# Left-over scores of an attention kernel: one form for all batches, and another place in the first batch

## The chip, the cores and the metric

The kernel runs on one core of a Trainium2 chip. The metric is the device time of that core in microseconds, as the median of several runs. One execution was also recorded by the hardware profiler; it is the profiled execution of the tables and quoted lines below. Times inside it are counted from the start of its span.

## The reference

Attention with a relative position bias, followed by a feed-forward layer with three first matrices whose products go through a maximum:

```python
scores = scale * np.matmul(q, k.transpose(0, 1, 3, 2))      # 8 batches, 8 heads, 576 x 64
scores = scores + bias.transpose(2, 0, 1)[None, :, :, :]     # a table's entry by |row - column|
scores = scores - np.max(scores, axis=-1, keepdims=True)
attn = np.exp(scores)
attn = attn / (np.sum(attn, axis=-1, keepdims=True) + 1e-09)
attn_out = np.matmul(attn, v)
x = attn_out.transpose(0, 2, 1, 3).reshape(B * S, H * D)     # 4608 x 512
h = np.maximum(np.maximum(x @ w1, x @ w2), x @ w3)           # 4608 x 768
out = h @ w_out
```

## The kernel before

**Units of work.** The eight heads are taken as four pairs (`hp`, 0 to 3). A head has 576 positions: four tiles of 128, and 64 left over. Scores are held transposed, with keys on the partitions. For a pair there are four pieces:

- *two visits* (`visit`, line 554), c = 0 for queries 0 to 255 and c = 1 for queries 256 to 511, each against the 512 keys of the four whole tiles. A visit makes two score tiles `sc`, and ACT turns each into a piece of `e4` with one exponential of 1024 columns (line 539);
- *the left-over keys* (`left_keys`, line 573): the last 64 keys of both heads against all queries, tile `sct`, into `el`;
- *the left-over queries*: the last 64 queries against the 512 keys, eight matmuls of 64 columns into `scq`, into the other part of `el`. There are two forms. `left_queries` (line 589) puts them in one tile of the pool `ps_s` and makes one exponential of 512 columns. A visit that is given `el` does them ahead of its own scores, in two tiles of the pool `ps_a`, with two exponentials of 256 columns.

The bias is multiplied in afterwards on DVE, as exp(bias): `times_band` for `e4`, `times_bandt` and `times_band_left` for `el`. Then `attend` (line 604) multiplies with the values, in two halves of the queries; the function that it returns does the division on DVE (`quotients`, lines 638 to 651) into `x_sb`. The list `late` holds the attends that are still to do, and `next_late` takes the first.

**Banks.** PSUM is split into three pools of two tiles each. `ps_s` (tiles of two banks) holds `sc`, `sct`, `scq` of the first form, and `tp` of `second_transposes`. `ps_a` holds the tiles of `attend`, and `scq` of the second form. `ps_f` holds the feed-forward tiles `ps` and `pso`, and the turnings `xp` and `tp2`. A new tile of a pool waits until what was in its place has been read.

**Order.** Matmuls and transposes are issued through helpers (lines 93 to 97) that keep them in program order on TensorE, so that one that waits holds up all behind it. Most DVE work is kept in order likewise. Feed-forward work for 512 tokens is cut into portions (`ffn`, line 317) in the list `pending`, and `fill(target, *hooks)` (line 439) issues portions whose sizes, in matmuls of 512 columns, sum to at most `target` (at least one portion), with the hooks between them: with one hook, it is called ahead of the last group; with two, they are spread. A portion of size 4 for the 256-token halves of batch 0 is eight matmuls of 256 columns, a block `ps`.

**Batch 0** runs in two passes over the pairs: first all visits c = 0, then (lines 758 to 810) all visits c = 1 with the left-overs and the bands. In this second pass the turnings of x (`x_transposes`, line 654: PE transposes into `xp`, one ACT copy to `xT`) make the transposed rows that the feed-forward work reads.

**Batches 1 to 7** (lines 813 to 894) do for each pair: visit c = 0; the attend of the first half of the pair before; a fill with the left-over keys; visit c = 1; a second fill. For batch 1 the turned queries and keys of the next pair are made by `second_transposes` (line 507) right after visit c = 1, as ten PE transposes into `tp` and four copies on DVE and ACT; later batches get them from the DMA queue of SP (`transposes`, line 454). The flag `together` (line 818) is true from batch 2, pair 1 on. Where it is true, the left-over queries are done in visit c = 1 (second form), the attend of the second half is done in the first fill right behind the left-over keys, and the first product of a block in the second fill takes its bank from `ps_a` (`idle_sums`, line 339). Where it is false, `left_queries` is called in the second fill, and the attend of the second half stands behind visit c = 1 (lines 860 to 863). `rate` is 8 for batch 1 and pair 0 of batch 2, and 13 after.

Of the kernel before, what the change touches and what calls it, by code (L numbers as in the profile page):

```python
# [39 lines left out]
def kernel(  # L40
# [19 lines left out]
    HP = H // 2  # L60
    QS = 2 * P
    QM = 2 * QS
# [28 lines left out]
    inorder = tc.keep_in_program_order  # L91
# [325 lines left out]
    pending, rest, stores, deferred, idle_sums = [], [], [], [], []  # L417
# [6 lines left out]
    def add_ffn(t0, nt, last=False):  # L424
        portions, left = ffn(t0, nt, last)
        portions[0] = rest + portions[0]
        rest[:] = left
        pending.extend((sum(n for n, _ in p), [fn for _, fn in p]) for p in portions)
# [10 lines left out]
    def fill(target, *hooks):  # L439

        groups, spent, hooks = [], 0, list(hooks)
        while pending and (not groups or spent + pending[0][0] <= target):
            n, fns = pending.pop(0)
            spent += n
            groups += [fn for fn in fns if fn]
        for j, group in enumerate(groups):
            while hooks and (j == len(groups) - 1 or j > 0 and len(hooks) > len(groups) - 1 - j):
                hooks.pop(0)()
            group()
        for hook in hooks:  # L450
            hook()
# [55 lines left out]
    def second_transposes(made, hp):  # L507

        hs = slice(2 * hp, 2 * hp + 2)
        tp = ps_s.tile([P, 2, 2 * CH], BF16, tag="sc", name="tp")  # L510
        for j, tl in enumerate((qtail, ktail)):
            for t in range(KT):
                tr(tp[:, j, P * t : P * t + P], batch[1][j][:, t, hs, :].rearrange("p h d -> p (h d)"), ident[:])
            tr(tp[:, j, KT * P : KT * P + P], tl[1][:, hp, :], ident[:])
        main = [
            copy(
                made[j][:, hp, 0 : KT * P].rearrange("c (p t) -> c p t", t=KT),
                tp[:, j, 0 : KT * P].rearrange("c (t p) -> c p t", t=KT),
            )
            for j, copy in enumerate((dve_copy, act_copy))  # L520
        ]
        tail = [
            copy(made[j][:, hp, KT * P :], tp[:, j, KT * P : n])
            for j, (copy, n) in enumerate(((dve_copy, S), (act_copy, (KT + 1) * P)))
        ]
        other_banks([main[1], tail[1]], [main[0], tail[0]])
        other_banks([tail[0]], [main[1]])

    def times_band(hp, e4, t, lo, hi, put=lambda x: x):
        lo, hi = max(lo, P * t - P), min(hi, P * t + 2 * P)  # L530
        if lo < hi:
            c0, c1 = BAND - (hi - P * t + P), BAND - (lo - P * t + P)
            put(nc.vector.tensor_tensor(  # L533
                out=e4[:, t, :, lo:hi], in0=e4[:, t, :, lo:hi],
                in1=hank[:, 2 * hp : 2 * hp + 2, c0:c1][:, :, ::-1], op=ALU.mult,
            ))
# [117 lines left out]
    def x_transposes(hp, half):  # L654

        xp = ps_f.tile([P, 2 * CH], BF16, tag="ff", name="xp")
        lo, hi = (0, QS) if half == 0 else (QS, S)
        for q in range(lo // P, -(-hi // P))[::-1]:
            c = min(P * q, S - P) - lo
            tr(xp[:, c : c + P], x_sb[0][:, q, P * hp : P * hp + P], ident[:])  # L660
        act_copy(xT[:, hp, lo:hi], xp[:, 0 : hi - lo])
# [8 lines left out]
    def next_late():  # L670
        return late.pop(0)() if late else (lambda: None)
# [9 lines left out]
    qk = [qk_tiles(), qk_tiles()]  # L681
# [45 lines left out]
    for hp in range(HP):  # L727
        qT, kT = (x[:, hp, :] for x in qk[0])
        e4, el = e_tiles()
# [28 lines left out]
    for hp in range(HP):  # L758
        qT, kT = (x[:, hp, :] for x in qk[0])
        e4, el = e_tiles()  # L760
        visit(qT, kT, e4, 1, (lambda: more_transposes(hp + 1)) if hp + 1 < HP else None)
        if hp == 0:
            bands(HP - 2)
            bands(HP - 1)
        if hp == 1:
            x_transposes(0, 0)
        if hp == 2:
            x_transposes(2, 0)
            x_transposes(3, 0)
            add_ffn(0, QS)  # L770

        def keys():
            left_keys(hp, qT, kT, el, QS, S)

        def queries():
            left_queries(hp, qT, kT, el)

        if hp == 0:
            keys()
            queries()  # L780
        quotients = next_late()

        def late_bands():
            for t in range(KT):
                times_band(hp, e4, t, QS, QM, inorder)

        if hp < 2:
            quotients()
            if hp == 1:
                keys()  # L790
            if hp == 1:
                x_transposes(1, 0)
            quotients = next_late()
            if hp == 1:
                queries()
            quotients()
            if hp == 0:
                make_bandt()
            late_bands()
            products(hp, el)  # L800
        else:
            if hp == HP - 1:
                batch[2] = load_tiles()
                load_qk(2)
                x_transposes(0, 1)
            quotients()
            late_bands()
            fill(8, keys, queries, *([lambda: second_transposes(qk[1], 0)] if hp == HP - 1 else []))
            products(hp, el)
        late.append(lambda hp=hp, e4=e4, el=el: attend(0, hp, e4, el, 1))  # L810

    turned = [lambda hp=hp: x_transposes(hp, 1) for hp in range(1, HP)]
    for b, hp in [(b, hp) for b in range(1, B) for hp in range(HP)]:
        if hp == 0:
            x_sb[b] = x_tile()
        qT, kT = (x[:, hp, :] for x in qk[b])
        e4, el = e_tiles()
        together = b > 1 and (b, hp) != (2, 0)
        rate = 8 if b == 1 or (b, hp) == (2, 0) else 13

        visit(qT, kT, e4, 0)
        store_outputs()
        if b == 1:
            if hp == 0:
                crossbar = transposes(2)
            next(crossbar, None)
        elif hp and b + 1 < B:
            if hp == 1:  # L830
                crossbar = transposes(b + 1)
            next(crossbar)
        early()
        if turned:
            turned.pop(0)()
        quotients = next_late()
        times_band(hp, e4, 0, 0, QS, inorder)
        quotients()
        if b == 1 and hp + 1 < HP:
            spread_packed(hp + 1, nc.vector)  # L840
        if (b, hp) == (1, 1):
            add_ffn(QS, QS)

        def keys():
            left_keys(hp, qT, kT, el, 0, S)
            if together:
                next_late()()

        fill(rate, keys, *([lambda: None] if together else []))
        times_bandt(hp, el)  # L850


        visit(qT, kT, e4, 1, el=el if together else None)
        store_outputs()
        if b == 1 or hp in (1, 2) and b + 1 < B:
            next(crossbar, None)
        early()
        if turned:
            turned.pop(0)()
        if not together:  # L860
            quotients = next_late()
            times_band(hp, e4, 1, 0, QM, inorder)
            quotients()
        if b == 1 and hp + 1 < HP:
            second_transposes(qk[1], hp + 1)
        if hp == 1 and b > 1:
            add_ffn((b - 1) * CH, CH)
        if hp == (2, 2, 0)[min(b, 3) - 1] and b + 1 < B:
            if b == 1:
                load_last_weights(turned_qk[2, 1, 1])  # L870
            load_v(b + 1, 0, H, turned_qk[b + 1, 1, KT - 1] if b < 3 else None)
        if (b, hp) == (2, 0):
            batch[3] = load_tiles()
            load_qk(3, divided[1, HP - 1, 1])
        if hp == 2 and 1 < b < B - 2:
            batch[b + 2] = load_tiles()
            load_qk(b + 2, turned_qk[b + 1, 1, KT - 1])

        def queries():
            if not together:  # L880
                left_queries(hp, qT, kT, el)
            times_band(hp, e4, 3, 0, QM, inorder)

        def bands_2():
            for t in range(1 if together else 2, 3):
                times_band(hp, e4, t, 0, QM, inorder)

        if together:
            idle_sums.append(hp)
        fill(rate, bands_2, queries)  # L890
        idle_sums.clear()
        times_band_left(hp, el)
        for half in range(2):
            late.append(lambda b=b, hp=hp, e4=e4, el=el, half=half: attend(b, hp, e4, el, half))
# [44 lines left out]
```

## Time and profile before

| What | Value |
|---|---|
| Median of 10 runs | 319.91 us (319.37 to 322.19) |
| The profiled execution | 319.97 us |
| Its span, first to last instruction | 318.2 us |
| Granted TensorE clock, mean of the span | 0.995 |
| PE, matmuls | 303.5 us busy, 95% |
| DVE | 213.5 us, 67% |
| ACT | 201.2 us, 63% |
| POOL | 108.2 us, 34% |
| One exponential of a score tile, 128 x 1024 | 1029 ns, 128 of them |

The page gives, for each engine, its busy time and a row of 40 digits, the busy share of 40 equal slices of the span in tenths (one slice is 8 us). The chain that ended last follows the work back from the last instruction. In the timeline a row has its start, how long it took from first to last, the engine and line, what it writes and reads (out<-in), the shape, the number of instructions merged into it, and in brackets idle time before it with what ended it. Matmuls overlap in such rows, so two starts tell more than the duration. In rows of windows come the stretch, its length, the busy time of PE, weight loads, DVE, ACT and POOL, then the granted clock of TensorE, the share of DMA and the rate.

Where the pieces lie: the second pass of batch 0 from about 20 to 35 us, batch 1 from 34.7, batch 2 from 62.5, its pair 1 from 68.6 and its pair 2 from 75.6 us.

### The profile page before, as it was taken

How to read it: one execution, taken by the hardware profiler on the slowest of the kernel's cores; microseconds unless marked ns; L12 is line 12 of the kernel's file. 1: busy time of each engine (PE TensorE's matmuls, PEld its weight loads, DVE VectorE, ACT ScalarE, POOL GpSimd, SP SyncE). 2: the span in 40 equal slices, each digit the busy share in tenths (PEclk: the TensorE clock that was granted, in tenths of full speed). 3: DMA queues.
4: the chain of work that ended last, by engine and by line, in shares of the span. 5: the costliest groups of instructions: out<-in, count | busy, mean ns of one | idle time of the engine just before them, and what ended most of it. 6: DMA issues, size and time to landing. Idle time of an engine off the chain costs nothing.

```text
span 318.2 us, 8198 instructions
## 1 busy us (share of the span) xinstructions
PE 303.5 (95%) x3288; PEld 171.4 (54%) x3328; DVE 213.5 (67%) x535; ACT 201.2 (63%) x297; POOL 108.2 (34%) x143
## 2 busy tenths in 40 slices
PE   7778999999999999999999999999999999999995
PEld 2356777775555555555555555555555555444442
DVE  7476778777666766666666777767767775553552
ACT  4868988886777667767777677767776741122221
POOL 8948731447079502940195058300000000000000
PEclk9979999999999999999999999999999999999999
DMA  9999999999999999999999999994032103302103
GB/s 165 177 214 201 181 150 132 148 106 167 235 124 141 135 202 128 132 110 197 151 130 136 216 139 140 123 192 108 10 69 99 36 2 74 134 0 75 58 0 132
DMA packets 163878, 40.34 MB, mean 127 GB/s; under 512 B 153720, under 2 KB 159360, under 8 KB 163840
## 3 DMA queue, kind: packets, MB, share of 16 engines
q0 software_dynamic: 103776, 16.66, 79.4%
q1 hardware_dynamic: 58304, 22.69, 39.5%
q10 hardware_dynamic: 1760, 0.47, 0.7%
q8 instruction: 26, 0.43, 0.6%
q14 instruction: 12, 0.10, 0.1%
HBM read 35.39 MB, written 9.45 MB: 141 GB/s over the span
## 4 chain that ended last, share of the span: by engine, by line
PE 73%; issue 1%; DMA 1%; ACT 1%
PE ps L94 39%; PE pso L94 13%; PE a L94 11%; PE sc L94 7%; PE sct L94 2%; PE scq L94 2%; DMA out_dram<-osb 1%; ACT e L539 0%; ACT osb L388 0%; ACT osb L107 0%
## 5 line engine op out<-in xcount | busy, mean ns | idle before, releaser
L94 PE MATMUL ps<-xT,w_bf 128*128 128x512 bf16 (+1 forms) x693 | 148.7, 357 | 1.4
L539 ACT ACTIVATE e<-sc 128x1024 bf16<-128x1024 f32 x128 | 124.4, 1029 | 20.0 <-PE sc L94 17.5
L94 PEld LDWEIGHTS <-w_bf 128*128 128x128 bf16 x720 | 65.3, 98 | 62.7 <-issue 5.0
L533 DVE TENSOR_TENSOR e<-e,hank 128x512 bf16<-128x512 bf16 (+2 forms) x136 | 58.6, 467 | 12.1 <-ACT e L539 9.9
L345 ACT ACTIVATE m<-ps 128x512 bf16<-128x512 f32 x48 | 29.2, 608 | 51.9 <-PE ps L94 51.9
L354 DVE TENSOR_TENSOR m<-ps,m 128x512 bf16<-128x512 f32 x48 | 33.1, 689 | 34.1 <-PE ps L94 34.0
L94 PEld LDWEIGHTS <-kT 64*128 64x128 bf16 (+1 forms) x832 | 29.9, 95 | 36.8 <-issue 23.9
L94 PE MATMUL pso<-wo_bf,hT 128*128 128x512 bf16 (+2 forms) x209 | 47.8, 373 | 0.8 <-issue 0.2
L94 PE MATMUL a<-vx,e 128*128 128x65 bf16 x1024 | 45.9, 195 | 0.0
L360 DVE TENSOR_TENSOR hT<-ps,m 128x512 bf16<-128x512 f32 x48 | 33.0, 689 | 15.9 <-PE ps L94 14.4
L94 PE MATMUL sc<-qT,kT 64*128 64x256 bf16 x512 | 40.8, 272 | 2.9 <-ACT e L539 1.3
L94 PEld LDWEIGHTS <-e 128*128 128x128 bf16 x1024 | 41.6, 99 | 0.8
L167 POOL DMA_DIRECT2D q_sb<-in_q_dram x24 | 22.0, 918 | 49.8 <-DMA qT<-qtail 16.0
L94 PE MATMUL a<-vt,el 128*128 128x130 bf16 x160 | 35.8, 224 | 0.2 <-DMA vt<-in_v_dram 0.2
L139 POOL DMA_DIRECT2D vx<-in_v_dram x32 | 28.4, 914 | 22.0 <-PE ps L94 18.9
L110 DVE COPY osb<-pso 128x512 f32<-128x512 f32 (+1 forms) x33 | 22.6, 686 | 17.9 <-PE pso L94 14.7
L539 ACT ACTIVATE el<-scq 128x256 bf16<-128x256 f32 (+1 forms) x55 | 20.5, 416 | 19.7 <-PE scq L94 19.6
L641 DVE TENSOR_TENSOR x_sb<-a,rd 128x256 bf16<-128x256 f32 (+1 forms) x64 | 31.4, 491 | 2.2
L94 PEld LDWEIGHTS <-hT 128*128 128x128 bf16 x222 | 20.2, 98 | 22.3 <-issue 1.5
L94 PEld LDWEIGHTS <-el 128*128 128x128 bf16 x416 | 24.2, 97 | 9.4 <-issue 5.5
L539 ACT ACTIVATE el<-sct 128x576 bf16<-128x576 f32 (+2 forms) x36 | 21.7, 607 | 5.6 <-PE sct L94 4.2
L167 POOL DMA_DIRECT2D k_sb<-in_k_dram x24 | 22.0, 917 | 1.1 <-DMA w_bf<-in_moe_w_dram 1.1
(71 smaller groups left out, 168.9 us busy)
## 6 DMA issues: line engine op xcount, KB each, us to landing
out_dram<-osb SPq DMA_DIRECT2D x35, 256.0 KB, 3.1
vx<-in_v_dram POOLq DMA_DIRECT2D x32, 128.0 KB, 8.2
q_sb<-in_q_dram POOLq DMA_DIRECT2D x26, 128.0 KB, 5.4
k_sb<-in_k_dram POOLq DMA_DIRECT2D x24, 128.0 KB, 5.7
w_bf<-in_moe_w_dram POOLq DMA_DIRECT2D x3, 768.0 KB, 10.0
xT<-in_k_dram SPq DMA_DIRECT2D x6, 128.0 KB, 5.0
hank<-w_dr SPq DMA_DIRECT2D x2, 384.0 KB, 6.7
wo_bf<-in_moe_w_out_dram POOLq DMA_DIRECT2D x1, 768.0 KB, 8.2
```

What stands on the lines that cost most here:

```text
L94: inorder(nc.tensor.matmul(*args, **kw))
L110: return inorder(nc.vector.tensor_copy(out_, in_))
L139: in_turn(b, nc.gpsimd.dma_start(out=dst[:, t, h0:h1, :], in_=x[:, t, h0:h1, :])) for t in range(t0, t1)
L167: loads.append(in_turn(b, nc.gpsimd.dma_start(out=dst[:, t], in_=main_part(src, b)[:, t])))
L345: nc.scalar.activation(out=st[fb]["m0"][:], in_=ps0, func=ACTF.Copy)
L354: inorder(nc.vector.tensor_tensor(out=m[:], in0=ps1, in1=st[fb]["m0"][:], op=ALU.max))
L360: inorder(nc.vector.tensor_tensor(out=block(fb), in0=ps2, in1=other, op=ALU.max))
L533: put(nc.vector.tensor_tensor(out=e4[:, t, :, lo:hi], in0=e4[:, t, :, lo:hi], in1=hank[:, 2 * hp : 2 * hp + 2, c0:c1][:, :, ::-1], op=ALU. ...
L539: nc.scalar.activation(out=out_, in_=in_, func=ACTF.Exp, scale=inv_sqrt_d)
L641: divided[b, hp, half] = inorder(nc.vector.tensor_tensor(out=x_sb[b][:, 2 * half : 2 * half + n, P * hp : P * hp + P].rearrange("p t (h d) ...
```

## The change

In batch 0's second pass: for pair 1, the left-over queries are done right behind the left-over keys, ahead of the turning of x and the attend that stood between. For pairs 2 and 3, left-over keys and queries leave the fill and come right behind the attend, ahead of the bands, of the turnings of x, and of the added feed-forward work (pair 2) or the loads of batch 2 (pair 3).

In batches 1 and 2: the flag `together` is gone, and what it stood for is done for all pairs. So batch 1, and pair 0 of batch 2, do the left-over queries in visit c = 1, and the attend of the second half in the first fill. The band of tile 1 (`times_band(hp, e4, 1, ...)`) moves from behind visit c = 1 to the hook of the second fill. The first fill of batch 2, pair 1, has the target 8 instead of 13.

```diff
@@ second pass of batch 0
-        if hp == 1:
-            x_transposes(0, 0)
-        if hp == 2:
-            x_transposes(2, 0)
-            x_transposes(3, 0)
-            add_ffn(0, QS)
...
         if hp == 0:
             keys()
             queries()
+        if hp == 1:
+            x_transposes(0, 0)
         quotients = next_late()
...
         if hp < 2:
             quotients()
             if hp == 1:
                 keys()
-            if hp == 1:
+                queries()
                 x_transposes(1, 0)
             quotients = next_late()
-            if hp == 1:
-                queries()
             quotients()
...
         else:
+            keys()
+            quotients()
+            queries()
+            late_bands()
+            if hp == 2:
+                x_transposes(2, 0)
+                x_transposes(3, 0)
+                add_ffn(0, QS)
+                fill(8)
+            else:
-            if hp == HP - 1:
                 batch[2] = load_tiles()
                 load_qk(2)
                 x_transposes(0, 1)
-            quotients()
-            late_bands()
-            fill(8, keys, queries, *([lambda: second_transposes(qk[1], 0)] if hp == HP - 1 else []))
+                fill(8, lambda: second_transposes(qk[1], 0))
             products(hp, el)
@@ batches 1 to 7
-        together = b > 1 and (b, hp) != (2, 0)
...
         def keys():
             left_keys(hp, qT, kT, el, 0, S)
-            if together:
-                next_late()()
+            next_late()()
 
-        fill(rate, keys, *([lambda: None] if together else []))
+        fill(8 if (b, hp) == (2, 1) else rate, keys, lambda: None)
         times_bandt(hp, el)
-        visit(qT, kT, e4, 1, el=el if together else None)
+        visit(qT, kT, e4, 1, el=el)
...
-        if not together:
-            quotients = next_late()
-            times_band(hp, e4, 1, 0, QM, inorder)
-            quotients()
...
         def queries():
-            if not together:
-                left_queries(hp, qT, kT, el)
             times_band(hp, e4, 3, 0, QM, inorder)
 
         def bands_2():
-            for t in range(1 if together else 2, 3):
+            for t in range(1, 3):
                 times_band(hp, e4, t, 0, QM, inorder)
 
-        if together:
-            idle_sums.append(hp)
+        idle_sums.append(hp)
```

More of the change, by code (lines that the diff above doesn't have):

```diff
@@ L776, in queries, with late_bands @@
             left_queries(hp, qT, kT, el)
+        def late_bands():
+            for t in range(KT):
+                times_band(hp, e4, t, QS, QM, inorder)
         if hp == 0:
@@ L780 @@
             queries()
+        if hp == 1:
+            x_transposes(0, 0)
         quotients = next_late()
-        def late_bands():
-            for t in range(KT):
-                times_band(hp, e4, t, QS, QM, inorder)
         if hp < 2:
```

## The prediction

> **What bounds the kernel now.** I read the page first, for the engine that is busy to the end and for the stretch in which it is not full.
>
> ```profile
> span 318.2 us, 8198 instructions
> ...
> PE 303.5 (95%) x3288; PEld 171.4 (54%) x3328; DVE 213.5 (67%) x535; ACT 201.2 (63%) x297; POOL 108.2 (34%) x143
> ...
> PE   7778999999999999999999999999999999999995
> ...
> ACT  4868988886777667767777677767776741122221
> ...
> PE 73%; issue 1%; DMA 1%; ACT 1%
> ```
>
> TensorE is the bound: nine tenths or more from 32 us on, and the chain that ended last is PE for 73% of the span, unbroken from 75 us. No later wait would hide a microsecond lost or won before that. Everything that the diff touches lies between 22 and 76 us, where ACT is nearly as full as PE. So I took the timeline of PE through it, and looked for starts further apart than the matmuls between them explain. A matmul of 64 rows by 256 columns runs beside its partner, and a pair takes 0.11; a 256-column `ps` takes 0.11, a transpose 0.06.
>
> ```profile
> 37.61 0.39 PE L94 MATMUL sc<-qT,kT 64*128 64x256 bf16 x4
> 38.19 0.40 PE L94 MATMUL sc<-qT,kT 64*128 64x256 bf16 x4 [0.19 <-ACT el L539]
> ...
> 52.87 0.66 PE L94 MATMUL sc<-qT,kT 64*128 64x256 bf16 x8
> ...
> 54.87 0.22 PE L97 MATMUL tp<-ident,ktail 128*128 128x128 bf16 x1
> 55.29 0.29 PE L94 MATMUL scq<-qT,kT 64*128 64x64 bf16 x8 [0.20 <-ACT e L539]
> 55.51 1.05 PE L94 MATMUL ps<-xT,w_bf 128*128 128x256 bf16 x8
> 56.49 0.61 PE L94 MATMUL sc<-qT,kT 64*128 64x256 bf16 x8
> ```
>
> Two kinds of loss show. First, waits for one of the two tiles of the pool ps_s: at 38.19 (0.58 after a group of two pairs, so 0.36 lost), again at 45.66 (0.35), at 55.29 (0.26 beyond the step named next), and three of 0.04. Second, a step each time TensorE goes from 128-row to 64-row matmuls and back: 0.10 in, 0.10 out. The left-over queries `scq` stand alone between 128-row work, and so pay both.
>
> The form that the change gives to batch index 1 and to pair 0 of batch 2 already runs from batch 2, pair 1. Its first instance, PE and then ACT:
>
> ```profile
> 73.56 0.29 PE L94 MATMUL scq<-qT,kT 64*128 64x64 bf16 x8
> 73.68 0.60 PE L94 MATMUL sc<-qT,kT 64*128 64x256 bf16 x8
> ...
> 75.62 0.39 PE L94 MATMUL sc<-qT,kT 64*128 64x256 bf16 x4
> 76.42 0.39 PE L94 MATMUL sc<-qT,kT 64*128 64x256 bf16 x4 [0.41 <-ACT e L539]
> ```
>
> ```profile
> 73.88 0.66 ACT L539 ACTIVATE el<-scq 128x256 bf16<-128x256 f32 x2 [1.76 <-PE scq L94]
> 74.42 3.78 ACT L539 ACTIVATE e<-sc 128x1024 bf16<-128x1024 f32 x4
> ```
>
> Call s the start of `scq`. The two `scq` exponentials hold ACT until s+0.86; the score exponentials follow, 0.91 apart and 1.03 long. So the visit's first ps_s tile is free at s+1.93 and its second at s+2.86 (76.42, exactly where PE waited). PE has issued the visit by s+0.66 (in the later batches, 89.95 to 90.61). **Whatever next needs a ps_s tile must have 1.27 us of other matmuls ahead of it, or PE waits.** Later batches put 2.7 us of feed-forward there. The stretch of the change does not.
>
> **The change part by part**, as PE time against the profiled execution.
>
> 1. *What joining saves.* Five visits (four of batch 1, one of batch 2) lose a pair of steps in and out: a lone `scq` takes 0.33 of PE (0.10 in, 48.42 to 48.65 behind), a joined one 0.13: 5 x 0.20 = **-1.00**. The `scq` tile leaves ps_s, so the waits at 38.19, 45.66, 55.29 and the three small ones go: 0.36+0.35+0.26+0.12 = **-1.09**. Two exponentials of 256 hold ACT 0.54 where one of 512 held it 0.49; that is in s+0.86. The scores now also wait for both ps_a tiles, so for the division of the second half's attend just ahead; DVE ends it about 0.9 after the attend, while `ps` and its step take 0.97. I take 0; 0.2 a visit if that cover is gone.
>
> 2. *The turnings behind the second visit, pairs 0 to 2 of batch 1.* Before, the second half's attend (0.90) stood between the visit and `second_transposes`. It moves to the first fill; its instructions cost the same there. Now `tp`, which needs a ps_s tile, is next at s+0.66 and waits until s+1.93: 1.27 twice, and 1.09 for pair 0, where the turning of x (0.18) lies between: **+3.63**. Queued behind it on PE are all feed-forward blocks of that fill and the next visit. DVE and ACT only have the copies of `tp` waiting, which come in time: ACT ends them at s+3.5, the next visit starts at s+3.5 at the earliest.
>
> 3. *Two visits with one block of 4 behind them: pair 3 of batch 1, pair 0 of batch 2.* The block ends at s+0.66+0.97 = s+1.63. The next visit's first tile waits until s+1.93 (0.30), its second half, due 0.22 later, until s+2.86 (0.71): 1.01 each, **+2.02**. Before, the attend and the lone `scq` filled this.
>
> 4. *The first fill of batch 2, pair 1, falls from 13 to 8.* One of its two `pso` blocks (1.28) moves behind the second visit. There the wait at 76.42 (due at 75.84) is covered: **-0.58**. The keys then follow the attend directly at about 1.15 after the visit, with the first tile free at 1.07: nothing.
>
> 5. *Batch 0, second pass, pairs 1 and 2.* Pair 1's `scq` fills the wait for the xT copy at 24.4, but is no longer beside the next visit: 0.1 earlier. In pair 2, the waits at 26.23 (0.2) and 27.45 (0.8 start to start) go: the attend, keys and queries give DVE time for the qT copy of 27.08. But the turnings of x now come behind the two left-over exponentials on ACT: these end about 28.6, the two xT copies at 28.9 and 29.2, and the first feed-forward block can't start before 28.95, where it starts at 28.91 now. **+0.05**: one wait for another.
>
> 6. *Pair 3.* The visit ends at 30.5, the attend at 31.4; keys wait for the first exponential (31.6: 0.2) and queries for the second (32.5: 0.7). Before, the x turning and a block (1.07) lay in between. Only the wait at 33.20 (0.4) goes: **+0.55**. `load_qk(2)`, eleven issues on POOL of 0.9, is moved past keys and queries too; POOL's first one waited for a `tp` of 33.7, so it may slide by half a microsecond. Its data are turned by SP until 57.1 and wanted at 62.5: hidden by 5 us. The x_sb turnings that SP issues with batch 1's last divisions move ahead of a visit, and are wanted at 80.
>
> Sum: -1.00 -1.09 +3.63 +2.02 -0.58 +0.05 +0.55 = **+3.58**. The profiled execution took 319.97 (span 318.2 and 1.8 around it), 0.06 above the median 319.91. DVE being late or early by 0.1 in places I can't settle; I forecast **323.4**, own range 322.3 to 324.4.
>
> **Two rules weighed.** The row: two `scq` exponentials in 0.54. The Trainium skill, Perfetto Trace Analysis, section Optimizing Scalar/DVE Operations, advises breaking up instructions when an unsaturated ScalarE causes bubbles elsewhere. By it the split should help: a ps_a bank is free 0.27 sooner, at most 5 x 0.27 = 1.3, giving 322.1. But nobody in the rows waits for that bank; what PE waits for is the score exponential behind. I take the row.
>
> The second speaks against the change. TensorE: Matmul & The Clock Gate, table Why this matters for your kernels, warns of PE idle gaps over about 3 us. No new wait passes 1.3, so by the rule the clock stays full. The trace is stricter:
>
> ```profile
> 17.79 0.30 PE L94 MATMUL sct<-qT,kT 128*128 128x320 bf16 x1 [0.80 <-ACT e L539]
> 18.70 0.29 PE L94 MATMUL scq<-qT,kT 64*128 64x64 bf16 x8 [0.62 <-ACT e L539]
> ```
>
> ```profile
> 18.00:19.00 1.00, 0.37 (x9) 0.26 (x8) 1.00 (x5) 0.98 (x2) 0.71 (x2) 0.98 1.19 214
> 19.00:20.00 1.00, 0.78 (x13) 0.78 (x14) 1.00 (x5) 0.60 (x1) 0.65 (x2) 0.50 1.20 224
> ```
>
> After idle times of 0.80 and 0.62 the granted clock (third figure from the end) was 0.50, until about 22.4. That cost up to 1.7 us of matmuls. Around each new wait of step 2 PE would still be busy for half of 3 us, and 24 to 28 us, at 2.75 busy of 4, kept 1.00. I leave a drop out of the sum and keep it as a rival.
>
> **Rivals.**
>
> - *Faster: the ps_s waits of steps 2 and 3 do not come about.* All rests on them, at the tiles that `tp` and the next visit take. For it: the same joined visit runs from 80 us without a wait, and the rest of the sum is -2.07. If score exponentials went ahead of those of `scq`, or a free tile were found, each wait shrinks; below 0.41 on average over the five visits, the change breaks even, and at none it gives 317.9. Against: 76.42 shows the wait with even more work behind the visit (1.28), and matmuls are kept in program order.
> - *No change, 319.0 to 320.9:* DVE and ACT catch up in the longer first fill and shorten the five waits to about 0.4. ACT's idle times there are 0.2 to 0.8 a visit; but no exponential can start before its scores exist.
> - *Slower still: the clock drops once,* +1.2 to +1.7, about 325.
> - *A smaller loss, 320.9 to 322.3:* step 6 doesn't show and the split pays as the rule says.
> - *The change doesn't do what it says:* the moved parts have their order written out; I see no way.
>
> **How the numbers follow.** The measurement tells a change from none at about 0.3%, 1.0 us. The forecast has 0.65, the clock drop 0.12, the smaller loss 0.06, no change 0.06, faster 0.11: slower 0.83, same 0.06, faster 0.11. The range leaves out faster, no change, and the tail beyond one drop: 321.0 to 325.2.
>
> **What would show it.** `tp` of batch 1 waiting about 0.9 to 1.3 for ACT e, three times; waits of PE sc for ACT e up to 0.7 at the starts of batch 2's pairs 0 and 1; none at pair 2. `scq` beside `sc` throughout batch 1. In batch 0, pair 3, `scq` waiting 0.7 for ACT e, and in pair 2 the first `ps` for ACT xT. The first visit of batch 2, pair 2, about 3.6 later, the rest of the trace shifted by as much. I am wrong if `tp` finds its tile free, or if the shift is made up after 80 us.

## The result

| | before | changed |
|---|---|---|
| Median | 320.22 us (52 runs) | 324.14 us (15 runs) |
| Ratio, 95% interval | | 1.0114, [1.0097, 1.0131] |
| Span of the profiled execution | 318.2 us | 321.8 us |
| Mean granted TensorE clock | 0.995 | 0.989 |

The changed kernel is slower by 1.1%: 3.65 us on 320.2, between 3.1 and 4.2. The ratio compares means, without two of the 52 runs that fell in a slower state of the chip; the medians alone would give 1.0122. The forecast was 323.4 against a median of 319.91, 3.5 us.

The page of the changed kernel, in the lines that answer to those of before:

```profile
span 321.8 us, 8204 instructions
...
PE 303.9 (94%) x3288; PEld 172.0 (53%) x3328; DVE 213.5 (66%) x535; ACT 201.4 (63%) x302; POOL 108.1 (34%) x143
...
PE   6978989889999999999999999999999999999995
...
ACT  4888787886777767776777677767775751121221
...
PEclk9699999999999999999999999999999999999999
...
PE 75%; issue 1%; DMA 1%; ACT 1%
```

The work is the same: as many matmuls, as many DVE instructions, five exponentials more on ACT, and busy times within 0.6 us. PE is merely less full: slices 6, 8 and 9 fall from 9 to 8. Who waited there is told by the waits of PE from 20 to 82 us, first of the kernel before, then of the changed one (total, times, longest):

```profile
PE xp L97 <- ACT xT L107: 0.6, 1, 0.6
PE xp L97 <- DVE qT L110: 0.6, 1, 0.6
PE sc L94 <- ACT el L539: 0.6, 3, 0.2
PE sc L94 <- ACT e L539: 0.4, 1, 0.4
PE tp L97 <- ACT el L539: 0.3, 1, 0.3
PE scq L94 <- ACT e L539: 0.2, 1, 0.2
PE pso L94 <- issue: 0.2, 1, 0.2
```

```profile
PE tp L97 <- ACT e L539: 3.3, 3, 1.2
PE sc L94 <- ACT e L539: 1.5, 4, 0.5
PE scq L94 <- ACT e L539: 1.4, 3, 0.6
PE ps L94 <- ACT xT L107: 0.6, 1, 0.6
PE scq L94 <- DVE x_sb L641: 0.3, 1, 0.3
```

Eight waits of 0.2 to 0.6 went. Three turnings and four score groups of batches 1 and 2 now wait for exponentials, and so do three `scq` in batch 0. The timeline of the changed kernel's PE shows a turning and two score groups: pair 1 of batch 1, and the visit behind pair 3.

```profile
46.98 0.36 PE L94 MATMUL scq<-qT,kT 64*128 64x64 bf16 x8
47.16 0.62 PE L94 MATMUL sc<-qT,kT 64*128 64x256 bf16 x8
48.98 0.38 PE L97 MATMUL tp<-ident,q_sb 128*128 128x128 bf16 x4 [1.21 <-ACT e L539]
...
63.23 0.36 PE L94 MATMUL scq<-qT,kT 64*128 64x64 bf16 x8
63.41 0.62 PE L94 MATMUL sc<-qT,kT 64*128 64x256 bf16 x8
63.96 1.05 PE L94 MATMUL ps<-xT,w_bf 128*128 128x256 bf16 x8
65.24 0.39 PE L94 MATMUL sc<-qT,kT 64*128 64x256 bf16 x4 [0.23 <-ACT e L539]
66.15 0.39 PE L94 MATMUL sc<-qT,kT 64*128 64x256 bf16 x4 [0.52 <-ACT e L539]
```

The turning starts at s+2.00, the two score groups at s+2.01 and s+2.92, where s is the start of `scq`; the forecast had s+1.93 and s+2.86.

**Legs.** To see small parts I cut each trace into legs, from the first score group of one pair's visit to that of the next pair (c = 1 in batch 0, c = 0 after; where a wait parts the two score groups of a visit in batches 1 and 2, the second one's start less 0.22). Most legs whose code is not touched repeat within 0.02 us from trace to trace, far better than whole executions do (the exception is batch 0's pair 2, which read 4.52 to 4.95 with the same code). One reason why executions differ lies behind 95 us: in three of the 14 traces (e1, e10, e11) PE waits once, for 1.0 to 1.3, for turned keys from the DMA queue.

| Leg, us | before | forecast | changed |
|---|---|---|---|
| batch 0, pair 2 | 4.52 | 4.57 | 4.64 |
| batch 0, pair 3 | 4.85 | 5.40 | 5.40 |
| batch 1, pair 0 | 7.59 | 8.12 | 8.63 |
| batch 1, pair 1 | 7.31 | 8.03 | 8.07 |
| batch 1, pair 2 | 6.87 | 7.64 | 7.66 |
| batch 1, pair 3 | 6.04 | 6.81 | 6.88 |
| batch 2, pair 0 | 6.04 | 6.81 | 6.85 |
| batch 2, pair 1 | 7.62 | 7.04 | 7.06 |

The forecast column is the leg of before with the terms of the sum put where they belong. The changed legs sum to 4.35 more. The span grew by only 3.6, since batch 0's pair 2 began 0.7 sooner in this profiled execution: its opening, the same code, had its half-clock stretch elsewhere. Nor is 4.35 the loss of the other runs, whose interval ends at 4.2: pair 0 of batch 1 reads 8.25 in e6 and e11, where its `scq` does not wait so long, and with that the sum is 4.0. From batch 2's pair 3 on, both traces take 233.2.

### The profile page after: what moved, and what is told of

It is laid out like the page before. It is cut to its first block, busy times and chain, and to the rows that moved or that the text cites. A ratio compares the mean times of both kernels' runs of the same rounds, so it can differ in the third digit from the quotient of the medians.

```text
span 321.8 us, 8204 instructions
## 1 busy us (share of the span) xinstructions
PE 303.9 (94%) x3288; PEld 172.0 (53%) x3328; DVE 213.5 (66%) x535; ACT 201.4 (63%) x302; POOL 108.1 (34%) x143
## 4 chain that ended last, share of the span: by engine, by line
PE 75%; issue 1%; DMA 1%; ACT 1%
PE ps L94 39%; PE pso L94 14%; PE a L94 12%; PE sc L94 7%; PE sct L94 2%; PE scq L94 2%; DMA out_dram<-osb 1%; ACT e L539 0%; ACT osb L388 0%; ACT osb L107 0%
## 5 line engine op out<-in xcount | busy, mean ns | idle before, releaser
L94 PE MATMUL a<-vx,e 128*128 128x65 bf16 x1024 | 45.0, 193 | 0.0
L360 DVE TENSOR_TENSOR hT<-ps,m 128x512 bf16<-128x512 f32 x48 | 33.1, 689 | 15.9 <-PE ps L94 14.4
L94 PEld LDWEIGHTS <-e 128*128 128x128 bf16 x1024 | 40.7, 97 | 0.8
```

Source lines behind the costliest of these rows:

```text
L94: inorder(nc.tensor.matmul(*args, **kw))
L360: inorder(nc.vector.tensor_tensor(out=block(fb), in0=ps2, in1=other, op=ALU.max))
```

## The experiments

**One part at a time.** Four kernels start from the kernel before. The first has only the diff of batch 0's second pass. The others:

```diff
 # e2_join_three
-        together = b > 1 and (b, hp) != (2, 0)
+        together = b > 1 and (b, hp) != (2, 0) or b == 1 and hp < 3
 # e3_join_two
-        together = b > 1 and (b, hp) != (2, 0)
+        together = b > 1 or (b, hp) == (1, 3)
 # e4_fill8_only
-        fill(rate, keys, *([lambda: None] if together else []))
+        fill(8 if (b, hp) == (2, 1) else rate, keys, *([lambda: None] if together else []))
```

> The kernel before with only the second pass of batch 0 changed. Theory (waits for score tiles and for the xT copies): step 5 nothing, step 6 a wait of 0.2 for the keys and 0.7 for the queries of pair 3 in place of 0.4: slower than before by 0.6 us (0.4 to 0.8). Rival (the loss is the clock: the trace after has 6.8 us at half clock, before 3.4): this part costs nothing, within 0.3 us.

> The kernel before with only pairs 0 to 2 of batch 1 joined. Theory: three turnings wait 1.1, 1.3 and 1.3 for the first score tile (+3.6), 0.5 for the division that the scq of pair 0 waited for in the trace after, less 0.6 of mode steps and 1.0 of waits that go: slower by 2.5 us (2.0 to 3.0). Rival (the split exponentials load ACT): three more exponentials at 0.05 each, less the same savings: faster by 1 us or more.

> The kernel before with only pair 3 of batch 1 and pair 0 of batch 2 joined. Theory: the visits behind them wait 0.3 and 0.7 for the two score tiles, 2.0 in all, less 0.4 of mode steps and 0.1 of small waits: slower by 1.5 us (1.2 to 1.9). Rival (split exponentials load ACT): faster by 0.4 us.

> The kernel before with only the first fill of batch 2, pair 1, at 8. Theory: the wait of 0.58 behind its second visit goes; its keys, now right behind the attend, are due at 0.6 after the visit and find the first tile 1.0 after it, so 0.4 comes back: faster by 0.2 us, too little for these rounds to tell from no change. The prediction's step 4 taken alone would say 0.6.

| Run | Ratio to before, 95% interval | us of it | Legs that it changes |
|---|---|---|---|
| e1_pass_only | 1.0007, [0.9986, 1.0028] | +0.2 | +0.12, +0.55 |
| e2_join_three | 1.0060, [1.0039, 1.0081] | +1.9 | +0.67, +0.76, +0.79 |
| e3_join_two | 1.0042, [1.0022, 1.0061] | +1.3 | +0.79, +0.82 |
| e4_fill8_only | 0.9999, [0.9979, 1.0018] | 0.0 | -0.17 |

The times of e1 and e4 tell nothing apart from no change; their legs are what was expected. e2 and e3 are slower where the rival had them faster, so joining itself costs there, by about the amounts of steps 2 and 3. The legs of the four kernels, 0.67 + 2.22 + 1.61 - 0.17, give 4.3 against 4.35, but that they agree so well is chance. The fill earns 0.56 in the changed kernel and 0.17 alone, where its keys find their tile not yet free; and pair 0 loses 1.04 in the profiled execution of the changed kernel and 0.67 in e2. The two differences cancel.

**Is the loss idle time, or work?** e11 puts useless work of 0.85 us where PE is said to wait.

```diff
         visit(qT, kT, e4, 1, el=el)
+        if b == 1 or (b, hp) == (2, 0):
+            idle = ps_f.tile([P, CH], F32, tag="ff", name="idle")
+            for _ in range(4):
+                mm(idle[:], lhsT=ident[:], rhs=w_bf[0][:, 0, 0:CH])
```

> The changed kernel with four useless matmuls of 512 columns, 0.85 us, behind the second visit of each of the five newly joined pairs: 4.3 us of work more on TensorE. Theory: it all lies in the waits of 1.1 to 1.3 and 1.0: no slower than the changed kernel, within 0.5 us. Rival (TensorE is full there and the loss is in its own work or clock): slower by 4.3 us.

Ratio to before 1.0106, [1.0072, 1.0140]; the changed kernel had 1.0114. The five legs read 8.25, 8.07, 7.66, 6.88, 6.85: 4.3 us of matmuls more, and none of the five longer; the leg behind them grew by 0.27. The timeline at pair 1 of batch 1:

```profile
48.17 0.62 PE L94 MATMUL sc<-qT,kT 64*128 64x256 bf16 x8
48.72 1.04 PE L94 MATMUL idle<-w_bf,ident 128*128 128x512 bf16 x4
49.99 0.38 PE L97 MATMUL tp<-ident,q_sb 128*128 128x128 bf16 x4 [0.24 <-ACT e L539]
```

The wait of 1.21 is 0.24 when four matmuls stand in it. That settles it: TensorE is not full there.

**Taking the first wait away.** e5 gives the turnings of pairs 1 to 3 of batch 1 two tiles of ps_a, which the `scq` exponentials free first:

```diff
-        tp = ps_s.tile([P, 2, 2 * CH], BF16, tag="sc", name="tp")
+        if hp:
+            tp = [ps_a.tile([P, 2 * CH], BF16, tag="a", name="tp") for _ in range(2)]
+        else:
+            tp = ps_s.tile([P, 2, 2 * CH], BF16, tag="sc", name="tp")
+            tp = [tp[:, j] for j in range(2)]
...
-        idle_sums.append(hp)
+        if b > 1:
+            idle_sums.append(hp)
```

> The changed kernel with the turnings tp of pairs 1 to 3 of batch 1 in two tiles of ps_a instead of one of ps_s (and the block of pair 0 that took a ps_a tile back in ps_f). The ps_a tiles are free when the two scq exponentials have ended, at s+1.0, not s+1.9. Theory: each of three waits shrinks by 0.9: faster than the changed kernel by 2.8 us, so about 0.9 us slower than before. Rival (turnings wait for something else, the copies or spread keys): no change from the changed kernel.

Ratio to before 1.0068, [1.0042, 1.0094]: about 1.5 us of the 3.65 came back, not 2.8. The turnings don't wait at all any more, yet only pair 1's leg fell as expected, 8.07 to 7.08. The waits of PE from 34 to 82 us:

```profile
PE sc L94 <- ACT e L543: 1.3, 3, 0.5
PE sc L94 <- ACT kT L107: 1.0, 1, 1.0
PE ps L94 <- ACT xT L107: 0.7, 1, 0.7
PE scq L94 <- DVE x_sb L645: 0.3, 1, 0.3
PE sc L94 <- DMA kT<-ktail: 0.2, 1, 0.2
```

The first row and the last are the waits of step 3, which e5 leaves alone. Two of the others stood as a second wait behind the first. Pair 2 has one block behind its turning, so the next visit comes early and waits 1.0 for the key copies, which stand behind both score exponentials on ACT. In pair 0 a block, which has given up its ps_a tile, waits 0.7 for the bank of the x turning, whose copy stands there too.

**The order on ACT.** e6 moved the call that issues the two `scq` exponentials behind the loop of the visit.

```diff
         if el is not None:
             ...
             turn_left_queries(qT, kT, banks)
-            put_left_queries(el, banks)
...
+        if el is not None:
+            put_left_queries(el, banks)
```

> The changed kernel with the two scq exponentials of a visit issued behind the two score exponentials, in all batches. Theory: the first score exponential starts 0.27 sooner (s+0.59, not s+0.86), so five waits shrink by 0.27: faster than the changed kernel by 1.3 us, if the ps_a tiles that scq then holds until s+3 are not wanted sooner; in batches 2 to 7 a block of each second fill takes a ps_a tile some 1.5 us behind the visit and would wait, some 1 us for each of about 20 pairs, which makes the whole slower by several us. Rival (the order on ACT does not matter): no change.

Ratio 1.0101, [1.0078, 1.0123]: no change, and nothing learned, for all 302 instructions of ACT ran in the same order as without the edit. The program does not hold exponentials in the order in which they are written, and the planner that schedules the program put them back. e10 holds them, in the five newly joined visits:

```diff
-            exp(e4[...], sc[:])
+            exp(e4[...], sc[:], inorder if first else lambda x: x)
...
+        if first:
+            put_left_queries(el, banks, inorder)
```

> The changed kernel with the score exponentials held ahead of the scq exponentials on ACT in the five newly joined visits (in e6 the planner put them back, so that run tested nothing). Theory: five waits for the first score tile shrink by 0.27, s+1.93 to s+1.66: faster than the changed kernel by 1.3 us; pair 2's next visit also waits for key copies on ACT, so 1.0 is the least. Rival (the order on ACT does not matter): no change.

Ratio 1.0107, [1.0072, 1.0141]: no gain, against 1.3 us expected. The turnings' wait did shrink (2.4 in all, from 3.3), and so did three legs, by 0.31, 0.36 and 0.31. But others grew: pair 2 waits 0.4 for key copies, now behind the `scq` exponentials too; a block in pair 0 waits 0.5 for a ps_a tile; the keys of batch 2, pair 1, wait 0.4. I had counted the gain of the mover and not who stands behind it.

**The division.** e7 puts the spreading (the DVE copies that lay out the packed q and k of batch 1 for the next pair) behind the second half's division.

```diff
             next_late()()
+            if b == 1 and hp + 1 < HP:
+                spread_packed(hp + 1, nc.vector)
```

> The changed kernel with the DVE spreading of packed q and k of batch 1 put behind the division of the second half in the first fill. Theory: the division ends 0.5 to 0.8 sooner, so the wait of scq for x_sb (0.5 start to start in pair 0) goes: faster than the changed kernel by 0.5 us. Rival (scq waits for the attend itself): no change.

Ratio 1.0116, [1.0090, 1.0141]: no difference in the time that 15 and 6 runs can tell. Pair 0's leg fell from 8.63 to 8.19, as expected, but it is 8.25 in e6 and e11, where the spreading stands as it did. So most of that wait comes and goes with the execution: e5 has it too, and there as in the changed kernel a copy of the spreading took over 0.6 (see the last section).

**A better version.** e8 is the kernel before with pairs 0 to 2 of batch 1 joined, the edits of e5 and e7, and the fill at 8.

> The kernel before with pairs 0 to 2 of batch 1 joined, their turnings in ps_a, the spreading behind the division, and the fill of batch 2, pair 1, at 8; pair 3 of batch 1, pair 0 of batch 2 and batch 0 as before. Theory: -0.6 of mode steps, -1.0 of waits, -0.2 of the fill, +0.3, +0.3 and +0.1 of turnings that wait for the scq exponentials: faster than before by 1.1 us (0.5 to 1.6). Rival (joining itself costs, whatever the tile): slower than before.

Ratio 1.0024, [0.9998, 1.0050]: a miss, some 0.8 us slower where 1.1 us faster was expected. Legs of pairs 0 to 2: 8.00, 7.08, 7.55, against 7.59, 7.31, 6.87 before; pairs 0 and 2 meet e5's second waits. e9 takes those copies off ACT, and fills two old waits:

```diff
-            for j, copy in enumerate((dve_copy, act_copy))
+            for j, copy in enumerate((dve_copy, dve_copy if hp == 3 else act_copy))
...
-        act_copy(xT[:, hp, lo:hi], xp[:, 0 : hi - lo])
+        copy = dve_copy if (hp, half) == (2, 1) else act_copy
+        copy(xT[:, hp, lo:hi], xp[:, 0 : hi - lo])
...
-        if hp == 2:
-            x_transposes(2, 0)
-            x_transposes(3, 0)
-            add_ffn(0, QS)
...
         quotients = next_late()
+        if hp == 2:
+            x_transposes(2, 0)
+            x_transposes(3, 0)
+            add_ffn(0, QS)
...
+            if (b, hp) == (2, 1):
+                next_late()()
             left_keys(hp, qT, kT, el, 0, S)
-            if together:
+            if together and (b, hp) != (2, 1):
                 next_late()()
...
```

> The kernel before with: in batch 0 pair 2 the attend ahead of the turnings of x (the order of keys and queries as before); pairs 0 to 2 of batch 1 joined, turnings in ps_a, spreading behind the division, the key copies of pair 2's turning and the x copy of pair 0 on DVE instead of ACT; the first fill of batch 2, pair 1, at 8 with its attend ahead of the keys. Theory, against before: -0.5 in batch 0, pair 2; -0.3, -0.2 and -0.3 in the three joined pairs (the copies on ACT were the second wait behind the turnings, so they must go too); -0.6 in batch 2, pair 1: faster by 1.9 us (1.2 to 2.3). Rival (the copies were not the second wait): pairs 0 and 2 stay 0.4 and 0.7 slower than before, and the whole is faster by 0.3 us at most.

Ratio 0.9950, [0.9917, 0.9984]: faster than before by 1.6 us. Legs: -0.59 in batch 0's pair 2, then 7.20, 7.10, 6.82, all below before, the last by only 0.05, since its visit waits 0.2 for the key copies, now on DVE. But its profile has a new wait, at the first attend of batch 2:

```profile
69.54 0.22 PE L94 MATMUL a<-vt,el 128*128 128x130 bf16 x1 [1.89 <-DMA vt<-in_v_dram]
```

The values of batch 2, which POOL loads behind SP's fourth pair of turnings, came later than PE. e12 sets them behind the third pair:

```diff
-            load_v(b + 1, 0, H, turned_qk[b + 1, 1, KT - 1] if b < 3 else None)
+            load_v(b + 1, 0, H, turned_qk[b + 1, 1, KT - 2 if b == 1 else KT - 1] if b < 3 else None)
```

> The kernel of e9 with the value loads of batch 2 set behind the third pair of SP's turnings instead of the fourth. In e9 the first attend of batch 2 waited 1.9 us for them. Theory: they start some 4 us sooner, that wait goes, and what e9 saves is seen: 0.5 in batch 0, 0.7 in the three joined pairs, 0.6 in batch 2, pair 1: faster than before by 1.9 us (1.2 to 2.5). Rival (the loads then hold up SP's last turnings, wanted by batch 2's first visit at 61): that visit waits instead, and the whole is no faster than e9.

Ratio 0.9965, [0.9939, 0.9991]: faster than before by 1.1 us, just under the range expected. The wait for the values is 0.2, and the leg of batch 2, pair 1, goes from 8.99 to 7.25. All eight legs together are 1.4 below before: 0.6 from the three joined pairs, 0.9 from the two old waits, less 0.15 elsewhere. e9 and e12 can't be told apart by their times. In e9's profiled execution the eight legs sum to 0.4 more than before, though its runs are 1.6 faster, so the wait of 1.89 is hardly in all of them. That e12's edit gains anything is not shown by times.

## Why the prediction was right

The mechanism was right, and the experiments show it. That 3.65 came so close to 3.58 is in part luck: the legs of the changed kernel's trace are 0.8 over the forecast, 0.5 of it in one pair, in a wait that comes and goes, and the interval is 1.1 wide.

- **What bounds the kernel:** right. PE's chain carries what is lost before 76 us to the end; the part behind takes 233.2 in both traces.
- **Step 1, savings:** the waits at 38.19, 45.66 and 55.29 are gone. The mode step was over-valued: `scq` to `sc` takes 0.18 in four of the five joined visits (46.98 to 47.16), where the instance that I read it from had 0.13. That is 0.05 for each. "I take 0" for the division was the term that failed: in pair 0 `scq` waited 0.5, start to start, in the profiled execution, 0.1 in e2. It is what lifts that leg from the 8.12 forecast to 8.63.
- **Step 2:** right in size: tiles free at s+2.0 for s+1.93, three waits as forecast. e11 shows that it is idle time, e5 that it is the tile. What I wrote of the copies, that ACT ends them at s+3.5, was right and more than an aside: it is the wait that e5 ran into.
- **Step 3:** right: at 63.96 the block begins, so the first score group was due at 64.93 and started at 65.24 (0.3), the second due at 65.46 and started at 66.15 (0.7). The legs grew by 0.84 and 0.81 against 0.77.
- **Step 4:** right within the changed kernel (-0.56), and only there; alone it gives 0.17.
- **Steps 5 and 6:** right in size, +0.12 for +0.05 and +0.55 for +0.55, with PE waiting for the xT copy and, in pair 3, for two score tiles where the text had it. But step 5 missed two waits of `scq` for a score tile, 0.48 in pair 1 and 0.29 in pair 2:

```profile
23.57 0.29 PE L94 MATMUL scq<-qT,kT 64*128 64x64 bf16 x8 [0.48 <-ACT e L539]
27.07 0.29 PE L94 MATMUL scq<-qT,kT 64*128 64x64 bf16 x8 [0.29 <-ACT e L539]
```

In pair 1 the wait stands in place of the old one for the xT copy; in pair 2 the leg is still only 0.12 longer. Pair 1, which no leg covers, takes 2.90 from its second score group to the next visit in both traces; the 0.1 that step 5 took off it doesn't show there.
- **The rule on breaking up instructions:** no gain from the split shows. Joined, the split exponentials stand ahead of the score exponentials, and the waits end when those end. No run has the joined form with one exponential, so what the split alone is worth stays open.
- **The clock:** the rival didn't come. The granted clock is 1.00 from 14.4 us to the last matmul, with three idle times of 0.9 to 1.2 in the stretch. The 15 timed runs of the changed kernel have a mean clock of 0.994, and the kernel before has 0.993 to 0.995 in its runs beside the experiments. So the rule of the Trainium skill (TensorE: Matmul & The Clock Gate, table Why this matters for your kernels) agrees with the trace for those idle times; its limit of about 3 us was not reached in any run here. That the trace was "stricter" was read from one execution. The idle times of 0.80 and 0.62 stand in all 14 traces, and in ten a half-clock stretch began within 1 us of the second one; in the other four (the changed kernel, e2, e9, e10) the clock stayed at 1.00 there. So they don't settle it, and what does, no run here explains.
- **The faster rival:** its break-even, waits of 0.41 on average, was far off; they were 1.1 to 1.3 and 1.0.

## What to carry to other kernels

Work that is moved away from behind a step may have been its cover: before joining, write down what the next instruction in order needs, when that comes free, and how much other work stands between. Fill the gap with useless work to learn whether it is idle. And when a wait is taken away, ask for the next one behind it: here it was copies in ACT's queue, then a load.

## What the runs showed of the hardware

A DVE copy of 128 x 512 bf16 within SBUF (the spreading, six in each trace) takes 0.28 us, or up to 0.75. In 14 traces 14 of the 84 took over 0.30, and all of them lie beside a DMA issue of POOL; so do 25 others, and none of the 45 without one took over 0.29. From the changed kernel, DVE and then POOL:

```profile
37.37 0.28 DVE L213 COPY q_sb<-xT 128x512 bf16<-128x512 bf16 x1
37.56 0.68 DVE L213 COPY k_sb<-xT 128x512 bf16<-128x512 bf16 x1
```

```profile
37.21 0.92 POOL L167 DMA_DIRECT2D q_sb<-in_q_dram  x1
38.12 0.89 POOL L167 DMA_DIRECT2D k_sb<-in_k_dram  x1
```

That copy is 0.4 late, and the division behind it is what `scq` of pair 0 waited for. Before, both took 0.28, with a POOL issue beside them as well, so a slow copy was seen only beside an issue, but not beside every one. The Trainium skill (SBUF — State Buffer, section Who interferes with whom) tells of a port pair that DVE and GpSimd share, as an exclusive lock; that fits, and no run here tested it.

The opening of the kernel, the same in all, had its half-clock stretch at 19 to 22 us in the trace before, at 8 to 14 in that of the changed kernel, and none after 16 us in a third (e2). Batch 0's pair 2 begins between 24.25 (e10) and 26.16 (e12), and so the spans of profiled executions differ where the legs don't.
